# Uneven token split in the first expert product of four chunks: 512, 384, 448 and 320 tokens in place of 288

## The chip, the cores and the metric

The kernel runs on one core of a Trainium2 chip (trn2). The metric is the device time of one execution in microseconds; two runs before the change took 1317.12 and 1317.86 us, with a median of 1317.49 us. Lower is better. The core has a matrix engine (TensorE, shown as PE, its weight loads as PEld), three engines for element-wise work (VectorE as DVE, ScalarE as ACT, GpSimd as POOL), and SyncE (SP), whose queue issues almost all transfers. Every engine works through its own list of instructions in order and waits on semaphores for the others.

## The reference

Attention runs twice per head: 32 pack queries `p` attend to the keys and values, and then every token attends to the 32 packed results. What comes out, `x` (4608 tokens of 512 features), goes through a dense mixture of four experts:

```python
p_packed = sm_attn(p, k, v)
out = sm_attn(q, p_packed, p_packed)
...
for e in range(E):                       # E = 4, F = 1024
    h = np.maximum(x @ w1[e], 0.0)
    out += p[:, e:e + 1] * (h @ w2[e])
```

There are 8 batches of 576 tokens, 8 heads of 64 features, and everything is float32.

## The kernel before, in words

**Precision.** All large products are done in the rounded float type `float32r`. A float32 operand is split into a high part (a rounded copy, made on ScalarE by `hi_of`, line 103) and a low part (the rest, made on GpSimd or VectorE by `lo_of`, line 108), and each product is the sum of three: high by low, high by high, low by high.

**Units.** The hidden dimension of each expert is cut in two, which gives 8 chunks (`ch`) of 512 hidden columns. Batches go in pairs (`sb` = 0 to 3). One unit is one chunk of one batch, so there are 64 units, in the order pair, chunk, batch. The change touches pair `sb == 2` (batches 4 and 5) in the odd chunks 1, 3, 5 and 7, thus 8 units.

**The first expert product.** The second attention and `w1` are fused: `g_form` multiplies the packed results with `w1` into `ghl` (stationary operand, 128 x 128 pieces), and the attention weights `xh`, `xl` (256 rows by 576 tokens) are the moving operand. `mm1_group(u, kh, c)` computes one quarter of a unit's hidden block: two slices of 128 hidden columns (`fi`) for one half of the tokens (`c`, 288 of 576), by 12 matmuls of 128 x 288 into one PSUM tile `dbl` (two banks, room for 512 columns in each). Then one VectorE instruction (line 310) takes the maximum with zero, multiplies by the expert's probability and writes the block `ablk`. The four blocks of a unit are named like a 2 by 2 matrix: `a11`, `a12` (first token half, first and second pair of hidden slices) and `a21`, `a22` (second token half).

**The second expert product.** It is a Strassen product of 2 by 2 blocks: seven products in place of eight. `ORDER` lists the left operands: `a11`, `s3`, `s1`, `s2`, `a22`, `s4`, `a12`, where s1 = a21 + a22, s2 = s1 - a11, s3 = a11 - a21 and s4 = a12 - s2. `s_operand` makes a sum on VectorE (`sblk`, line 327), its high part on ScalarE and its low part on GpSimd (`st`, four buffers). `product` does 12 matmuls of 128 x 288 with `st` moving and the prepared `w2` combinations `tt` stationary, and VectorE adds the result to the accumulator `acc` (line 392).

**Order of the work.** The loop over units emits, after each product i of unit u, the operand of the product two places ahead (`LA = 2`, so s1 of the next unit is emitted after product 0 of that unit), and the next unit's first product by the table GROUPS: group (0,0) after product 1, (0,1) after 3, (1,1) after 4, (1,0) after 6. Where a step of the attention of the next pair, or a `g_form`, is due, it stands between them. A scheduler then fixes the order on each engine from these priorities, so an instruction can stand earlier or later than it was emitted. PSUM has four `dbl` tiles, which products, groups, `g_form` and the attention share.

The loop that calls the function is this, cut to the calls in question:

```python
GROUPS = {1: ((0, 0),), 3: ((0, 1),), 4: ((1, 1),), 6: ((1, 0),)}
...
        for i in range(NPROD):
            product(u, i)
            n = i + LA
            if n < NPROD:
                s_operand(u, n)
            elif nxt:
                s_operand(u + 1, n - NPROD)
            if nxt:
                for grp in (GROUPS_LATE if u == 1 else GROUPS).get(i, ()):
                    mm1_group(u + 1, *grp)
```

Of the kernel before, what the change touches and what calls it, by code (L numbers as in the profile page):

```python
# [8 lines left out]
F32 = mybir.dt.float32  # L9
F32R = mybir.dt.float32r  # L10
AF = mybir.ActivationFunctionType
ALU = mybir.AluOpType
# [4 lines left out]
P = 128  # L17
B, H, S, D = 8, 8, 576, 64
# [5 lines left out]
HS = S // 2  # L24
# [14 lines left out]
def attention_moe(ctx: ExitStack, tc: tile.TileContext, q, k, v, p, dp, w1, w2, out):  # L39
    nc = tc.nc  # L40
# [24 lines left out]
    def mm(**kw):  # L65
        on_pe(nc.tensor.matmul(**kw))  # L66
# [15 lines left out]
    def dbl():  # L82
        return ps_dbl.tile([P, 2, 512], F32, name="dbl")
# [199 lines left out]
    pbt = {}  # L283
# [5 lines left out]

    blocks = {}  # L290

    def mm1_group(u, kh, c):
        sb, ch, b = units[u]
        xh, xl = xs[b]
        ts = slice(c * HS, (c + 1) * HS)
        ps = dbl()
        for fi in range(2):
            f = 2 * kh + fi
            fs = slice(f * P, (f + 1) * P)
            n = 0  # L300
            for g in range(NG):
                ghl = gs[b, ch][g]
                for hl, rx in ((0, xl), (0, xh), (1, xh)):
                    mm(
                        out=ps[:, fi, 0:HS], lhsT=ghl[:, hl, fs], rhs=rx[:, g, ts],
                        start=n == 0, stop=n == 3 * NG - 1,
                    )
                    n += 1
        a = hpool.tile([P, 2, HS], F32, name="ablk", bufs=6)
        nc.vector.scalar_tensor_tensor(  # L310
            out=a, in0=ps[:, :, 0:HS], scalar=0.0,
            in1=pbt[b][:, ts].rearrange("p (o t) -> p o t", o=1).broadcast_to([P, 2, HS]),
            op0=ALU.max, op1=ALU.mult,
        )
        blocks[u, f"a{c + 1}{kh + 1}"] = a

    def s_operand(u, i):

# [152 lines left out]
    hpool = ctx.enter_context(tc.tile_pool(name="hpool", bufs=1, reuse_waits="tile"))  # L471
    with ExitStack() as first:
# [30 lines left out]
        for kh, c in ((0, 0), (0, 1), (1, 1), (1, 0)):  # L503
            mm1_group(0, kh, c)
# [33 lines left out]
    for u, (sb, ch, b) in enumerate(units):  # L538
# [25 lines left out]
        for i in range(NPROD):  # L564
# [6 lines left out]
# [3 lines that stand above are left out]
# [66 lines left out]
```

## Time and profile before

| what | value |
|---|---|
| runs, median | 1317.12 and 1317.86 us, 1317.49 us |
| span of the profiled execution | 1316.5 us |
| TensorE matmul (PE) busy | 1271.3 us, 97% |
| VectorE (DVE) busy | 955.5 us, 73% |
| GpSimd (POOL) busy | 859.4 us, 65% |
| ScalarE (ACT) busy | 477.4 us, 36% |
| granted TensorE clock, mean | 0.989 |

The span is the time from the first to the last instruction in one execution that the hardware profiler recorded; the runs' times include what lies around it. A group row of the profile gives line, engine, operation, the tiles written and read, the shape, the count, then the busy time and the mean duration of one, then the engine's idle time just before such instructions and what ended it. Matmuls overlap one another, so the mean duration of one (about 0.3 us) is longer than the distance from one to the next. The third pair's units lie between about 702 us and 1015 us of the span.

### The profile page before, as it was taken

To read this page: it belongs to the slowest core of one execution; us is meant where nothing else is said; L and a number is where in the kernel's file an instruction comes from. 1 tells how busy PE (TensorE), PEld (TensorE's weight loads), DVE (VectorE), ACT (ScalarE), POOL (GpSimd) and SP (SyncE) were. 2 spreads that over 40 slices of the span, in tenths; PEclk is the share of its full clock that TensorE was granted. 3 is DMA by queue.
4 is the path that set the end of the run, shared out by engine and by line. 5 is a ranking of instruction groups with operands and counts; after the bars stand their busy time and mean duration, and the time that the engine had idled before them with its cause. 6 is when DMAs were issued, how large, how long until landed. Compare 5 with 4: busy or idle time off the path is not lost.

```text
span 1316.5 us, 26695 instructions
## 1 busy us (share of the span) xinstructions
PE 1271.3 (97%) x10720; PEld 1178.2 (89%) x10720; DVE 955.5 (73%) x1334; ACT 477.4 (36%) x786; POOL 859.4 (65%) x576
## 2 busy tenths in 40 slices
PE   3999999999899999999999999999999999999997
PEld 2789898888899989999999998999999999999997
DVE  5585777899894676888687566699669466666668
ACT  2445434343335332333334433233323533323231
POOL 4878888688886445557578554566558655555556
PEclk8899999999999999999999999999999999999999
DMA  9786556445365445554335645443446443335422
GB/s 323 275 298 225 205 172 220 169 143 187 127 204 164 167 139 174 174 184 131 123 111 194 202 156 182 132 135 118 154 138 206 151 137 118 117 129 154 129 97 73
DMA packets 89979, 218.42 MB, mean 166 GB/s; under 512 B 9088, under 2 KB 31744, under 8 KB 89856
## 3 DMA queue, kind: packets, MB, share of 16 engines
q1 hardware_dynamic: 89184, 216.57, 49.4%
q8 instruction: 86, 1.41, 0.4%
q14 instruction: 37, 0.30, 0.1%
q10 hardware_dynamic: 672, 0.15, 0.1%
HBM read 177.81 MB, written 38.87 MB: 165 GB/s over the span
## 4 chain that ended last, share of the span: by engine, by line
PE 83%; DVE 9%; POOL 3%; DMA 2%; issue 1%; ACT 0%; DVEq 0%; SPq 0%; ACTq 0%; POOLq 0%
PE dbl L66 78%; PE dbl L74 5%; DVE sblk L327 2%; DVE acc L392 1%; DVE ablk L310 1%; POOL tt L108 1%; DVE acc L442 1%; DVE acc L407 1%; DMA pnd<-pb 1%; PE dbl L69 1%; POOL st L108 1%; POOL acc L442 1%; DVE ghl L108 1%; DMA td<-tt 0%; DVE nb L166 0%
## 5 line engine op out<-in xcount | busy, mean ns | idle before, releaser
L66 PEld LDWEIGHTS dbl<-st,tt 128*128 128x128 f32 x5376 | 730.9, 189 | 66.1 <-issue 31.1
L66 PE MATMUL dbl<-st,tt 128*128 128x288 f32 x5376 | 774.7, 298 | 9.6 <-DVE acc L392 3.7
L108 POOL TENSOR_TENSOR st<-sblk,st 128x576 fp32r<-128x576 f32 x256 | 396.8, 1556 | 220.2 <-ACT st L103 216.4
L66 PE MATMUL dbl<-xh,ghl 128*128 128x288 f32 x2048 | 419.0, 296 | 2.1 <-DVE ghl L108 2.1
L108 POOL TENSOR_TENSOR st<-ablk,st 128x576 fp32r<-128x576 f32 x192 | 288.2, 1504 | 180.5 <-ACT st L103 172.2
L392 DVE TENSOR_TENSOR acc<-dbl,acc 128x576 f32<-128x576 f32 x385 | 289.0, 752 | 121.3 <-PE dbl L66 119.7
L66 PEld LDWEIGHTS dbl<-xh,ghl 128*128 128x128 f32 x2048 | 331.5, 189 | 3.4 <-DVE ghl L108 3.4
L66 PE MATMUL dbl<-xl,ghl 128*128 128x288 f32 x1024 | 304.7, 298 | 17.7 <-POOL xl L108 13.5
L310 DVE SCALAR_TENSOR_TENSOR ablk<-dbl,pbt 128x576 f32<-128x576 f32 x256 | 192.6, 753 | 172.3 <-PE dbl L66 171.8
L103 ACT CAST st<-sblk 128x576 fp32r<-128x576 f32 x256 | 173.1, 676 | 300.8 <-DVE sblk L327 210.4
L66 PEld LDWEIGHTS dbl<-xl,ghl 128*128 128x128 f32 x1024 | 193.8, 189 | 21.0 <-POOL xl L108 14.7
L103 ACT CAST st<-ablk 128x576 fp32r<-128x576 f32 x192 | 129.8, 676 | 224.3 <-PE dbl L66 214.0
L103 ACT CAST ghl<-dbl 128x512 fp32r<-128x512 f32 x128 | 74.6, 586 | 146.5 <-PE dbl L74 91.7
L327 DVE TENSOR_TENSOR sblk<-ablk 128x576 f32<-128x576 f32 x128 | 118.3, 925 | 9.3
L108 DVE TENSOR_TENSOR ghl<-dbl,ghl 128x512 fp32r<-128x512 f32 x128 | 87.5, 685 | 10.2 <-ACT ghl L103 6.5
L74 PE MATMUL dbl<-wraw,ppbd 64*32 64x512 f32 x1024 | 72.9, 600 | 0.0
L327 DVE TENSOR_TENSOR sblk<-ablk,sblk 128x576 f32<-128x576 f32 x64 | 65.3, 1020 | 6.6 <-POOL st L108 0.9
L108 POOL TENSOR_TENSOR tt<-b,tt 128x512 fp32r<-128x512 f32 x42 | 59.3, 1419 | 5.6 <-ACT tt L103 5.5
L442 POOL TENSOR_TENSOR acc<-acc,acc 128x576 f32<-128x576 f32 x28 | 47.4, 1704 | 18.1 <-DVE acc L392 18.1
L327 DVE TENSOR_TENSOR sblk<-sblk,ablk 128x576 f32<-128x576 f32 x64 | 56.5, 883 | 1.7
L390 ACT COPY acc<-dbl 128x576 f32<-128x576 f32 x56 | 35.9, 641 | 47.4 <-PE dbl L66 46.5
L442 DVE TENSOR_TENSOR acc<-acc,acc 128x576 f32<-128x576 f32 x21 | 31.6, 1507 | 4.9 <-POOL acc L442 4.6
(76 smaller groups left out, 420.3 us busy)
## 6 DMA issues: line engine op xcount, KB each, us to landing
tt<-td SPq DMA_DIRECT2D x182, 512.0 KB, 4.4
wraw<-in_w SPq DMA_DIRECT2D x136, 256.0 KB, 3.2
td<-tt SPq DMA_DIRECT2D x56, 512.0 KB, 3.7
pbt<-pnd SPq DMA_DIRECT2D x32, 288.0 KB, 4.4
out<-acc SPq DMA_DIRECT2D x32, 288.0 KB, 2.3
kt<-in_k SPq DMA_DIRECT2D x14, 576.0 KB, 5.0
kt<-in_q SPq DMA_DIRECT2D x14, 576.0 KB, 5.5
vt<-in_v SPq DMA_DIRECT2D x15, 512.0 KB, 5.5
```

The source lines that it names most:

```text
L66: on_pe(nc.tensor.matmul(**kw))
L69: on_pe(nc.tensor.transpose(**kw))
L74: ins = nc.tensor.matmul(**kw).ins
L103: nc.scalar.copy(out=dst, in_=src)
L108: eng.tensor_tensor(out=dst, in0=src, in1=hi.bitcast(F32), op=ALU.subtract)
L310: nc.vector.scalar_tensor_tensor(out=a, in0=ps[:, :, 0:HS], scalar=0.0, in1=pbt[b][:, ts].rearrange("p (o t) -> p o t", o=1).broadcast_to( ...
L327: nc.vector.tensor_tensor(out=t, in0=blk(x), in1=blk(y), op=op)
L390: nc.scalar.copy(out=accs[b, i], in_=psv)
L392: nc.vector.tensor_tensor(out=accs[b, i], in0=psv, in1=accs[b, i], op=ALU.add)
L407: nc.vector.tensor_tensor(out=dst, in0=x, in1=y, op=op)
L442: eng.tensor_tensor(out=m[dst], in0=m[x], in1=m[y], op=op)
```

## The change

`mm1_group` no longer cuts the 576 tokens at 288 in the 8 units of pair 2 with an odd chunk. A table gives the width of the first piece: 512 in chunk 1, 384 in chunk 3, 448 in chunk 5 and 320 in chunk 7; the second piece is the rest: 64, 192, 128 and 256 tokens. The number of matmuls stays at 12 for a group and 48 for a unit, and so does the sum of their columns. The blocks `a11` to `a22` stay cut at 288, since the second product needs them so. So a group of the wide piece now writes a whole block of the first token half and a part of one of the second, by two VectorE instructions, and a group of the narrow piece writes the rest of that second block.

```diff
+    FIRST = {1: 512, 3: 384, 5: 448, 7: 320}
+
     def mm1_group(u, kh, c):
         sb, ch, b = units[u]
         xh, xl = xs[b]
-        ts = slice(c * HS, (c + 1) * HS)
+        cut = FIRST.get(ch, HS) if sb == 2 else HS
+        ts = slice(0, cut) if c == 0 else slice(cut, S)
+        w = ts.stop - ts.start
         ps = dbl()
...
                     mm(
-                        out=ps[:, fi, 0:HS], lhsT=ghl[:, hl, fs], rhs=rx[:, g, ts],
+                        out=ps[:, fi, 0:w], lhsT=ghl[:, hl, fs], rhs=rx[:, g, ts],
                         start=n == 0, stop=n == 3 * NG - 1,
                     )
                     n += 1
-        a = hpool.tile([P, 2, HS], F32, name="ablk", bufs=6)
-        nc.vector.scalar_tensor_tensor(
-            out=a, in0=ps[:, :, 0:HS], scalar=0.0,
-            in1=pbt[b][:, ts].rearrange("p (o t) -> p o t", o=1).broadcast_to([P, 2, HS]),
-            op0=ALU.max, op1=ALU.mult,
-        )
-        blocks[u, f"a{c + 1}{kh + 1}"] = a
+        for half in range(2):
+            lo, hi = max(ts.start, half * HS), min(ts.stop, (half + 1) * HS)
+            if lo >= hi:
+                continue
+            name = f"a{half + 1}{kh + 1}"
+            if (u, name) not in blocks:
+                blocks[u, name] = hpool.tile([P, 2, HS], F32, name="ablk", bufs=6)
+            nc.vector.scalar_tensor_tensor(
+                out=blocks[u, name][:, :, lo - half * HS:hi - half * HS], in0=ps[:, :, lo - ts.start:hi - ts.start],
+                scalar=0.0, in1=pbt[b][:, lo:hi].rearrange("p (o t) -> p o t", o=1).broadcast_to([P, 2, hi - lo]),
+                op0=ALU.max, op1=ALU.mult,
+            )
```

The names in the following lists are the program's: `dbl` is a PSUM tile, `xl` and `xh` the attention weights, `st` a split operand, `acc` an accumulator, and `a` the attention weights on their way through the softmax. The changed file is 9 lines longer, so line 310 is now 320, 327 is 336 and 392 is 401.

**TensorE, first unit of chunk 1.** These rows are the end of group (0,0), two products and the start of group (0,1):

```order
L66 MATMUL dbl<-xl_6506,ghl 128x512
L66 MATMUL dbl<-xh_6505,ghl 128x512 x2
L66 MATMUL dbl<-st,tt 128x288 x24
L66 MATMUL dbl<-xl_6506,ghl 128x64
L66 MATMUL dbl<-xh_6505,ghl 128x64 x2
```

Before, the same rows stand in the same sequence, with 128x288 in all of them; the widths differ.

**VectorE, between the first two units of chunk 5 (batch 4).** Here VectorE also does the softmax of the next pair's token attention (lines 235 to 241). The `sblk<-ablk` row is s1, `sblk<-sblk,ablk` is s2, and `sblk<-ablk,sblk` is s4. Before:

```order
L392 TENSOR_TENSOR acc_8979<-dbl,acc_8979 128x576
L236 TENSOR_SCALAR s_11019<-s_11019 128x18
L327 TENSOR_TENSOR sblk<-ablk 128x576
L392 TENSOR_TENSOR acc_8999<-dbl,acc_8999 128x576
L236 TENSOR_SCALAR s_11187<-s_11187 128x18
L237 RECIPROCAL s_11019<-s_11019 128x18
L327 TENSOR_TENSOR sblk<-sblk,ablk 128x576
L310 SCALAR_TENSOR_TENSOR ablk<-dbl,pbt 128x576
```

Now:

```order
L238 TENSOR_TENSOR a_10894<-a_10894,s_11029 128x576
L238 TENSOR_TENSOR a_10897<-a_10897,s_11198 128x576
L241 STREAM_TRANSPOSE at<-a_10894 128x576
L320 SCALAR_TENSOR_TENSOR ablk<-dbl,pbt 128x576
L320 SCALAR_TENSOR_TENSOR ablk<-dbl,pbt 128x2x160
L401 TENSOR_TENSOR acc_8537<-dbl,acc_8537 128x576
L336 TENSOR_TENSOR sblk<-ablk 128x576
L401 TENSOR_TENSOR acc_8558<-dbl,acc_8558 128x576
L241 STREAM_TRANSPOSE at<-a_10897 128x576
L336 TENSOR_TENSOR sblk<-sblk,ablk 128x576
```

The sums s1 and s2 stood ahead of the write-out of group (1,0); they now stand behind both of its write-outs, and behind the two multiplications of line 238 and one transposition.

**GpSimd, the same place.** The `xl` rows are the low parts of the next pair's attention weights; the rows are, in this order, `a11`, s3, `xl2`, s1, `xl3` and s2. Now:

```order
L108 TENSOR_TENSOR st_10989<-ablk_10853,st_10989 128x576
L108 TENSOR_TENSOR st_11010<-sblk_11008,st_11010 128x576
L108 TENSOR_TENSOR xl2_10330<-at_11055,xh2_10329 128x576
L108 TENSOR_TENSOR st_11052<-sblk_11050,st_11052 128x576
L108 TENSOR_TENSOR xl3_10334<-at_11270,xh3_10333 128x576
L108 TENSOR_TENSOR st_11075<-sblk_11073,st_11075 128x576
```

Before, the two `xl` rows stood further on, behind s1, s2, `a22`, s4 and `a12`; each now precedes one of the sums.

## The prediction

> **What bounds the kernel now.** I read the page first: the busy shares, the chain of work that ended last, and the costliest groups.
>
> ```profile
> span 1316.5 us, 26695 instructions
> PE 1271.3 (97%) x10720; PEld 1178.2 (89%) x10720; DVE 955.5 (73%) x1334; ACT 477.4 (36%) x786; POOL 859.4 (65%) x576
> PE 83%; DVE 9%; POOL 3%; DMA 2%; issue 1%; ACT 0%; DVEq 0%; SPq 0%; ACTq 0%; POOLq 0%
> L66 PE MATMUL dbl<-xh,ghl 128*128 128x288 f32 x2048 | 419.0, 296 | 2.1 <-DVE ghl L108 2.1
> L66 PEld LDWEIGHTS dbl<-xh,ghl 128*128 128x128 f32 x2048 | 331.5, 189 | 3.4 <-DVE ghl L108 3.4
> ```
>
> TensorE is busy nearly all the time and makes up 83% of the chain, so a nanosecond added to each of its matmuls arrives at the end, and one that another engine needs does not, until TensorE waits for it. Next I took the busy time by stretch for the third pair. Each row has a stretch, its length, the busy time and the number of instructions on PE, PEld, DVE, ACT and POOL, then the granted clock, the share of the DMA engines and GB/s.
>
> ```profile
> 740.00:780.00 40.00, 40.00 (x386) 37.43 (x385) 26.90 (x43) 14.27 (x25) 19.80 (x15) 1.00 0.53 174
> 820.00:860.00 40.00, 40.00 (x372) 36.83 (x371) 28.85 (x45) 12.98 (x20) 18.99 (x13) 1.00 0.50 159
> 860.00:900.00 40.00, 40.00 (x339) 37.19 (x338) 36.68 (x55) 14.28 (x22) 26.41 (x17) 1.00 0.39 124
> 940.00:980.00 40.00, 40.00 (x317) 38.00 (x316) 26.80 (x37) 12.28 (x19) 21.75 (x16) 1.00 0.43 133
> ```
>
> Here TensorE is full at a granted clock of 1.00, and VectorE has about a third of its time free, except between 860 and 900 us, where the softmax of the next pair loads it to 36.68 of 40 us. So two questions decide: what a narrow and a wide matmul cost, and whether a later block makes TensorE wait, above all near 900 us.
>
> The distance between matmuls comes from the timeline, where each row has its start, its duration and a count.
>
> ```profile
> 800.45 0.19 PEld L66 LDWEIGHTS dbl<-xl,ghl 128*128 128x128 f32 x1 [0.34 <-DVE nb L167]
> 800.56 0.33 PEld L66 LDWEIGHTS dbl<-xh,ghl 128*128 128x128 f32 x2
> 809.63 1.76 PE L66 MATMUL dbl<-st,tt 128*128 128x288 f32 x12
> 803.25 0.77 PE L69 MATMUL dbl<-ident,a 128*128 128x128 f32 x5
> ```
>
> Twelve matmuls of 288 columns take 1.76 us, of which the last alone is 0.30, so one follows another after (1.76 - 0.30) / 11 = 0.133 us. A group of the first product is the same, 1.60 us. The two loads at 800.45 and 800.56, the first ones after a wait, stand 0.11 us apart: that is how long a 128 x 128 weight load of the rounded type keeps the load path. Every matmul here has its own load, so no matmul can follow sooner than 0.11 us after the one before, however few columns it has, unless loads go faster in a stream than in this pair.
>
> **The change, part by part.** *Matmuls.* Nothing is removed: per chunk 96 wide or narrow matmuls stand for 96 of 288 columns, 48 pairs. If the distance is a constant plus so much for each column, a pair costs the same for every cut, 2 x 0.133 = 0.266 us, and only the floor of 0.11 us under the narrow ones adds time. The price of a column has to be bounded, since all these matmuls have 288:
>
> ```profile
> L74 PE MATMUL dbl<-wraw,ppbd 64*32 64x512 f32 x1024 | 72.9, 600 | 0.0
> L74 PE MATMUL dbl<-kt,pt 64*32 64x288 f32 x224 | 10.7, 436 | 5.2 <-DMA kt<-in_k 5.2
> ```
>
> At most it is 133 / 288 = 0.46 ns. For plain float32 these rows give (600 - 436) / 224 = 0.73 ns; if the rounded type took half of that, 0.37 ns. I take 0.42, between the two. Then 64 columns would follow after 133 - 0.42 x 224 = 39 ns, 128 after 66, 192 after 93, and 256 after 120. With the floor at 110 the loss of a pair is 71 ns (chunk 1), 44 (chunk 5), 17 (chunk 3) and 0 (chunk 7), together 132 ns, times 48 = **+6.3 us**. With 0.46 or 0.37 a column it would be 7.3 or 5.3. Bounds of the floor: below, none at all, 0 us. Above, 133 ns for every narrow matmul (if the present distance were already that of the loads): 94 + 67 + 40 + 13 = 214 ns, times 48 = 10.3 us. I take 110, because a load's own distance is the nearest row.
>
> The Trainium skill, in "TensorE: Matmul & The Clock Gate", section "LDWEIGHTS (loading the stationary operand)", gives a load P / 1.2 ns for P columns, an estimate of 107 ns for 128, and the 0.11 us between the two loads agrees; by it the sum would be 5.9 us in place of 6.3.
>
> *Write-outs.* Each of the 8 units has two more VectorE instructions. What an instruction costs beside its elements I take from these:
>
> ```profile
> L225 DVE STREAM_TRANSPOSE a<-dbl 128x288 f32<-128x288 f32 x32 | 12.8, 451 | 2.9 <-PE dbl L74 2.9
> L241 DVE STREAM_TRANSPOSE at<-a 128x576 f32<-128x576 f32 x16 | 12.3, 769 | 3.6 <-POOL a L238 3.0
> ```
>
> 288 elements more cost 318 ns, so 451 - 318 = 133 ns is fixed. Sixteen times 0.13 is 2.1 us of VectorE, spread over stretches with 11 to 13 free us in 40: nothing, since VectorE's free time there covers it; without that cover it would be the 2.1 us.
>
> *The wait that is added.* Block `a22` was complete after group (1,1); now its larger part comes with group (1,0), after product 6. So s1 = a21 + a22 can be formed only then, and product 2 of the unit needs it, three TensorE pieces later (products 0 and 1 and a group). The least roomy of the ordinary places is chunk 7, batch 4:
>
> ```profile
> 977.13 0.76 DVE L310 SCALAR_TENSOR_TENSOR ablk<-dbl,pbt 128x576 f32<-128x576 f32 x1 [0.82 <-PE dbl L66]
> 981.08 1.44 POOL L108 TENSOR_TENSOR st<-sblk,st 128x576 fp32r<-128x576 f32 x1
> 981.71 2.56 PE L66 MATMUL dbl<-st,tt 128*128 128x288 f32 x18
> ```
>
> From 977.13: write-outs 0.76 and, for 2 x 32 elements, 0.2; s1 0.75; ScalarE 0.7 and GpSimd 1.44, with three hand-overs of 0.1: ready at 981.3, before 981.71, when product 2 starts. The others have at least a microsecond more. Near 900 us it is different. Queued ahead of s1 on VectorE are now both multiplications of line 238, one transposition, both write-outs and an accumulator sum:
>
> ```profile
> 899.25 0.73 DVE L235 TENSOR_REDUCE s<-a 128x18 f32<-128x576 f32 x1
> 900.65 0.74 DVE L327 TENSOR_TENSOR sblk<-ablk 128x576 f32<-128x576 f32 x1
> 903.69 1.15 DVE L238 TENSOR_TENSOR a<-a,s 128x576 f32<-128x576 f32 x1
> 905.43 1.32 DVE L327 TENSOR_TENSOR sblk<-ablk,sblk 128x576 f32<-128x576 f32 x1
> 906.67 1.99 DVE L238 TENSOR_TENSOR a<-a,s 128x576 f32<-128x576 f32 x1
> 909.25 0.76 DVE L241 STREAM_TRANSPOSE at<-a 128x576 f32<-128x576 f32 x1
> 906.10 1.95 POOL L108 TENSOR_TENSOR st<-ablk,st 128x576 fp32r<-128x576 f32 x1
> 906.65 1.63 PE L66 MATMUL dbl<-st,tt 128*128 128x288 f32 x11
> ```
>
> Before, s1 was formed at 900.65 and product 2 started at 906.65. Now TensorE reaches that product later by three wide groups less two narrow ones: 3 x 12 x 67 ns - 2 x 12 x 23 ns = 1.8 us, at 908.5. VectorE's queue begins 0.8 us later (one wide group) and loses 0.7 in the two narrow write-outs, so line 235 starts at about 899.4. Behind it come two sums and four small ones (0.66 + 0.67 + 0.67 + 0.5 = 2.5, to 901.9), two multiplications (1.15 each, or 1.15 and 1.99: 2.3 to 3.1), a transposition 0.7, write-outs 0.67 and 0.45, a sum 0.67, and s1 itself, 0.74 to 1.32: it ends between 907.4 and 908.8. ScalarE 0.8 and GpSimd 1.44 follow: ready between 909.7 and 911.1, a wait of 1.2 to 2.6 us, 1.9 in the middle. For s2, a second transposition on VectorE and `xl3` on GpSimd stand between: 1.4 us more at product 3. Together I take **+3.3 us**, between 0 (a queue that runs faster) and 6 (twice as slow).
>
> At the last changed unit VectorE waits for GpSimd's sums of the finished batch:
>
> ```profile
> 996.66 1.97 DVE L442 TENSOR_TENSOR acc<-acc,acc 128x576 f32<-128x576 f32 x1 [0.66 <-POOL acc L442]
> 998.56 0.74 DVE L310 SCALAR_TENSOR_TENSOR ablk<-dbl,pbt 128x576 f32<-128x576 f32 x1
> 1002.23 2.95 PE L66 MATMUL dbl<-st,tt 128*128 128x288 f32 x21
> ```
>
> 998.56 + 0.74 + 0.2 + s1 0.75 to 1.1 + ScalarE 0.8 + GpSimd 1.44 = 1002.5 to 1002.8, against 1002.23: **+0.5 us**.
>
> **The sum.** 1316.5 + 6.3 + 3.3 + 0.5 = 1326.6 us of span. The median of the runs stands 1.0 us above the profiled span (1317.5 against 1316.5), so the time is **1327.6 us**, 0.8% over the present one.
>
> **Rivals.** *No floor.* If weight loads run far enough ahead in a stream, the narrow matmuls cost what their columns cost, pairs stay at 0.266 us, and without a wait on s1 the time is 1317.5, not slower than before; with the wait 1321. For it: the queue already loads one matmul ahead. Against it: loads are busy 89% of the span, and the first pair of them already stands 0.11 us apart. It decides if the distance of 64-column matmuls is under 60 ns. The same page of the Trainium skill, section "Back-to-back issue gap", gives in a stream of load and matmul about 131 ns for 512 columns and 81 for 128; by that estimate the 512/64 pairs would cost at most 212 ns, 54 less than now, a gain of 2.6 us; but the trace has 133 ns at 288 columns already, so I count it as a small part of this rival's chance.
>
> *A slower rate for narrow matmuls.* Plain float32 shows that there is more than one rate: the five transpositions at 803.25 take (0.77 - 0.29) / 4 = 120 ns for 128 columns or less, 0.94 ns a column. If the rounded type fell to that below its present width, 192 columns would follow after 180 ns and 256 after 240, and 64 and 128 after 110 and 120: losses of 71 + 54 + 87 + 120 = 332 ns, times 48 = 15.9 us, thus 1317.5 + 15.9 + 3.8 = 1337. At twice that price a column, which no row excludes, the losses are 120 - 39 = 81, 240 - 66 = 174, 360 - 93 = 267 and 480 - 120 = 360 ns: 42 us, 1363; if 256 columns still ran at the present rate, 25 us, 1346, slower by over 2%. For it: no row shows a rounded matmul under 288 columns. Against it: nothing in the trace changes rate with width.
>
> *Loads bound everything.* Floor 133 ns: 10.3 in place of 6.3, so 1331.6.
>
> *The wait spreads.* If the late s1 delays the accumulator sums behind it until PSUM runs out, each of the 8 units loses a microsecond or two: 1327.6 + 8 = 1336. Against it: TensorE waits nowhere in the stretches above, and VectorE has a third of its time.
>
> **How the numbers follow.** Chances: forecast 0.50, loads bound everything 0.13, no floor 0.13, slower rate 0.18 (0.07 of it over 1343.8), the wait spreads 0.06. 2%, or 26 us, is about what a measurement of this kernel can tell from no change. All but the worst slower rates lie within it: faster 0.01, same 0.92, slower 0.07. The range 1319 to 1340 takes in the forecast with both bounds of its floor, the plain rate and the spreading wait; what it leaves out is the lower end of "no floor" and the upper end of "slower rate".
>
> **What would show each step.** In the changed profile the matmul groups on line 66 split by shape. Twelve 64-column matmuls should take about 1.3 us between their first and the next piece of work, as should those of 128 and 192; those of 256 about 1.44; of 512 about 2.7 (12 x 227 ns). TensorE should wait about 2 us before product 2 and 1 us before product 3 in chunk 5, batch 4, for GpSimd, and hardly anywhere else. I am wrong if the narrow groups take 0.5 us (no floor), if 192 columns take longer than 288 (slower rate), or if waits stand in all 8 units.

## The result, and the profile after

The changed kernel took 1329.58 and 1333.17 us, median 1331.38 us, against 1317.49 before: a ratio of 1.0106 (95% interval 1.0073 to 1.0139). Timed again in five rounds beside the kernel before (the ninth run below), the ratio was 1.0121 (1.0104 to 1.0138). So it is slower by about 1%, 14 to 16 us. The profiled execution is the one of 1333.17 us, with a span of 1331.3 us, 14.8 us over that of before.

The page's rows that answer to those of before:

```profile
span 1331.3 us, 26724 instructions
PE 1280.7 (96%) x10720; PEld 1182.4 (89%) x10720; DVE 959.4 (72%) x1350; ACT 476.9 (36%) x786; POOL 860.9 (65%) x576
PE 81%; DVE 11%; POOL 4%; DMA 1%; issue 1%; ACT 0%; DVEq 0%; SPq 0%; ACTq 0%; POOLq 0%
```

TensorE is busy for 9.4 us more, and VectorE and GpSimd have gained 2 and 1 points of the chain: TensorE now also waits more. Where the time went is seen from the starts of the same product in the timelines of both kernels. The table gives the start of product 0 of the first unit of a stretch, and what the stretch took. The groups of a chunk run one unit ahead of its products, so each stretch begins before the chunk: that of chunk 1 with the last unit of chunk 0 (three units in all), the others with the first unit of the even chunk before (four units). The column "swapped" is the first experiment below.

| stretch holding the cut of | starts before, after | before | after | swapped | distances alone |
|---|---|---|---|---|---|
| everything ahead | 0, 0 | 722.05 | 719.72 | 719.38 | 0 |
| chunk 1 (512/64) | 722.05, 719.72 | 59.62 | 63.77 | 63.15 | +3.7 |
| chunk 3 (384/192) | 781.67, 783.49 | 81.35 | 82.27 | 82.27 | +0.9 |
| chunk 5 (448/128) | 863.02, 865.76 | 76.38 | 84.67 | 78.88 | +2.5 |
| chunk 7 (320/256) | 939.40, 950.43 | 75.60 | 79.41 | 76.53 | +0.05 |
| after the pair | 1015.00, 1029.84 | 301.5 | 301.5 | 301.6 | 0 |

So the pair itself took 17.2 us more (4.15 + 0.92 + 8.29 + 3.81), and 2.3 us were given back ahead of it, nearly all by chance, as shown further down. The last column is what the new distances between matmuls make of it. They are read from rows like these, of the wide and the narrow group of chunk 1 (a row holds one or two matmuls, and the starts of equal rows are three matmuls apart):

```profile
723.71 0.39 PE L66 MATMUL dbl<-xl,ghl 128*128 128x512 f32 x1
723.93 0.63 PE L66 MATMUL dbl<-xh,ghl 128*128 128x512 f32 x2
724.40 0.39 PE L66 MATMUL dbl<-xl,ghl 128*128 128x512 f32 x1
...
729.22 0.28 PE L66 MATMUL dbl<-xl,ghl 128*128 128x64 f32 x1
729.33 0.39 PE L66 MATMUL dbl<-xh,ghl 128*128 128x64 f32 x2
729.55 0.28 PE L66 MATMUL dbl<-xl,ghl 128*128 128x64 f32 x1
```

With 512 columns three matmuls take 724.40 - 723.71 = 0.69 us, 230 ns each; with 64 columns 0.33, 110 ns each. Over all groups the median distances are 231 (512), 207 (448), 173 (384), 147 (320), 120 (256), 111 (192), 112 (128) and 112 ns (64). The pairs lose 77, 53, 18 and 1 ns, times 48: 7.15 us in all. Nearly all of the other 10 us lies in two places.

**Chunk 5, batch 4.** The stages there, with the granted clock behind the busy times:

```profile
909.00:912.00 3.00, 2.77 (x15) 2.20 (x14) 3.00 (x4) 1.35 (x2) 1.54 (x2) 1.00 0.36 97
912.00:915.70 3.70, 1.80 (x12) 1.57 (x12) 3.09 (x5) 2.42 (x4) 3.70 (x3) 1.00 0.00 0
917.30:921.00 3.70, 3.70 (x23) 3.16 (x30) 1.20 (x3) 0.67 (x1) 3.70 (x3) 0.50 0.00 0
921.00:924.00 3.00, 3.00 (x24) 1.76 (x9) 1.48 (x2) 0.80 (x2) 0.17 (x1) 0.52 0.17 61
924.00:928.00 4.00, 4.00 (x35) 4.00 (x34) 1.94 (x4) 1.04 (x2) 1.42 (x1) 1.00 0.26 86
```

TensorE idles for 1.9 of the 3.7 us from 912, and then runs at half clock from 917 to 924 us, 6.8 us long. The timeline says what it waited for, and what half clock does:

```profile
908.39 1.21 DVE L336 TENSOR_TENSOR sblk<-ablk 128x576 f32<-128x576 f32 x1
910.46 1.43 POOL L108 TENSOR_TENSOR st<-sblk,st 128x576 fp32r<-128x576 f32 x1 [1.48 <-ACT st L103]
910.88 1.63 DVE L336 TENSOR_TENSOR sblk<-sblk,ablk 128x576 f32<-128x576 f32 x1
911.85 1.95 POOL L108 TENSOR_TENSOR xl<-at,xh 128x576 fp32r<-128x576 f32 x1
911.95 1.85 PE L66 MATMUL dbl<-st,tt 128*128 128x288 f32 x12 [0.23 <-POOL st L108]
912.62 0.68 ACT L103 CAST st<-sblk 128x576 fp32r<-128x576 f32 x1 [0.96 <-DVE sblk L336]
913.77 1.92 POOL L108 TENSOR_TENSOR st<-sblk,st 128x576 fp32r<-128x576 f32 x1
915.74 2.22 PE L66 MATMUL dbl<-st,tt 128*128 128x288 f32 x12 [1.94 <-POOL st L108]
917.76 0.31 PE L66 MATMUL dbl<-xl,ghl 128*128 128x128 f32 x1
918.30 0.41 PE L66 MATMUL dbl<-xl,ghl 128*128 128x128 f32 x1
918.94 0.41 PE L66 MATMUL dbl<-xl,ghl 128*128 128x128 f32 x1
920.35 1.96 PE L74 MATMUL dbl<-wraw,ppbd 64*32 64x512 f32 x16
```

Product 2 (911.95) waits shortly for the low part of s1, and product 3 (915.74) nearly 2 us for that of s2. The `xl` row on GpSimd holds this one up by only about 0.5 us, since ScalarE has the high part of s2 done at 913.30. The rest is that s2 itself is formed late on VectorE (910.88), and that the sum takes 1.63 us and its low part 1.92, in place of the usual 0.74 and 1.43. Then three matmuls of 128 columns take 918.94 - 918.30 = 0.64 us in place of 0.33, and the sixteen matmuls of line 74 take 1.96 in place of 1.09.

**Chunk 7, batch 5.** Here s1 is not what is late. The matmul shown is the sixth of the next pair's first group, the first that needs the low part of the second `ghl`. Before the change, then after it:

```profile
999.41 1.14 DVE L327 TENSOR_TENSOR sblk<-ablk,sblk 128x576 f32<-128x576 f32 x1
1000.47 0.68 DVE L108 TENSOR_TENSOR ghl<-dbl,ghl 128x512 fp32r<-128x512 f32 x1
1001.20 0.40 PE L66 MATMUL dbl<-xh,ghl 128*128 128x288 f32 x1 [0.29 <-DVE ghl L108]
```

```profile
1009.00 1.07 DVE L336 TENSOR_TENSOR sblk<-ablk 128x576 f32<-128x576 f32 x1
1010.11 1.88 DVE L336 TENSOR_TENSOR sblk<-sblk,ablk 128x576 f32<-128x576 f32 x1
1012.09 1.77 DVE L336 TENSOR_TENSOR sblk<-ablk,sblk 128x576 f32<-128x576 f32 x1
1013.79 0.68 DVE L108 TENSOR_TENSOR ghl<-dbl,ghl 128x512 fp32r<-128x512 f32 x1
1014.52 0.40 PE L66 MATMUL dbl<-xh,ghl 128*128 128x288 f32 x1 [2.45 <-DVE ghl L108]
```

Before, only s4 stood directly ahead of that low part, and TensorE waited 0.29 us. Now VectorE does s1, s2 and s4 one after another, the last two at more than twice the usual 0.74 us while GpSimd works beside it, and only then the low part of `ghl`, for which TensorE waits 2.45 us. Half clock follows again, 3.4 us from 1016.0.

**The 2.3 us ahead of the pair.** Half clock explains 2.05 of these. Two stretches of the kernel before, then the same two of the changed kernel:

```profile
330.00:335.70 5.70, 2.63 (x16) 2.19 (x17) 5.70 (x7) 2.98 (x5) 5.70 (x5) 1.00 0.00 0
335.70:339.20 3.50, 3.50 (x17) 3.50 (x17) 2.71 (x5) 1.17 (x2) 2.84 (x3) 0.51 0.44 169
```

```profile
330.00:335.70 5.70, 2.63 (x18) 2.20 (x18) 5.70 (x7) 2.98 (x5) 5.70 (x5) 1.00 0.00 0
335.70:339.20 3.50, 3.50 (x28) 3.50 (x27) 3.07 (x5) 1.93 (x3) 3.50 (x3) 1.00 0.39 147
```

In both kernels TensorE idles alike at 330 us, in the first pair, which the change doesn't touch; in the execution of before the clock then halved, and in the changed one it did not. It cost 2.05 us there. The code ahead of the pair is the same in every run of this document, and in all 13 profiled executions TensorE idles for 2.7 us at one go there; half clock followed in nine of them and not in four. So this difference is chance, and not the change.

### The profile page after: what moved, and what is told of

Same layout as the page of the kernel before. It is cut to its first block, busy times and chain, and to the rows that moved or that the text cites. A ratio compares the mean times of both kernels' runs of the same rounds, so it can differ in the third digit from the quotient of the medians.

```text
span 1331.3 us, 26724 instructions
## 1 busy us (share of the span) xinstructions
PE 1280.7 (96%) x10720; PEld 1182.4 (89%) x10720; DVE 959.4 (72%) x1350; ACT 476.9 (36%) x786; POOL 860.9 (65%) x576
## 4 chain that ended last, share of the span: by engine, by line
PE 81%; DVE 11%; POOL 4%; DMA 1%; issue 1%; ACT 0%; DVEq 0%; SPq 0%; ACTq 0%; POOLq 0%
PE dbl L66 76%; PE dbl L74 5%; DVE sblk L336 3%; POOL st L108 2%; DVE acc L401 1%; DVE ablk L320 1%; POOL tt L108 1%; DVE acc L416 1%; PE dbl L69 1%; DMA pnd<-pb 1%; POOL acc L451 1%; DVE acc L451 1%; DVE a L238 0%; DVE ghl L108 0%; DVE nb L166 0%
## 5 line engine op out<-in xcount | busy, mean ns | idle before, releaser
L66 PE MATMUL dbl<-xh,ghl 128*128 128x288 f32 (+4 forms) x2048 | 424.5, 299 | 4.3 <-DVE ghl L108 4.3
L66 PE MATMUL dbl<-xl,ghl 128*128 128x288 f32 (+4 forms) x1024 | 306.7, 300 | 19.5 <-POOL xl L108 14.7
L320 DVE SCALAR_TENSOR_TENSOR ablk<-dbl,pbt 128x576 f32<-128x576 f32 (+4 forms) x272 | 193.7, 717 | 174.7 <-PE dbl L66 174.2
L336 DVE TENSOR_TENSOR sblk<-ablk,sblk 128x576 f32<-128x576 f32 x64 | 68.1, 1065 | 5.6 <-POOL st L108 0.5
L103 ACT CAST tt<-b 128x512 fp32r<-128x512 f32 x42 | 25.2, 618 | 26.6 <-DVE b L373 11.4
```

The lines of the kernel that those rows point to most:

```text
L103: nc.scalar.copy(out=dst, in_=src)
L320: nc.vector.scalar_tensor_tensor(out=blocks[u, name][:, :, lo - half * HS:hi - half * HS], in0=ps[:, :, lo - ts.start:hi - ts.start], scal ...
L336: nc.vector.tensor_tensor(out=t, in0=blk(x), in1=blk(y), op=op)
```

## The experiments

My theory after the result: about 7 us are the floor that the weight load sets under narrow matmuls; the rest are sums that are formed too late in two places, and the half clock that follows the waits. The rivals: the widths cost all of it in some way; the additional write-outs load VectorE; the half clock comes from something else.

**Swapped pieces.** The narrow piece first, so that a22 is again complete after group (1,1).

```diff
         cut = FIRST.get(ch, HS) if sb == 2 else HS
+        cut = S - cut
         ts = slice(0, cut) if c == 0 else slice(cut, S)
```

> The same four cuts with the pieces swapped: the narrow piece comes first (64, 192, 128, 256 tokens in groups (0,0) and (1,0)), the wide one second. Matmul widths, their count and the number of write-outs are those of the change, but a22 is again complete after group (1,1). Theory (floor of the weight load 7.2 us, the rest late sums and the clock that falls after them): 7.2 us over the kernel before, about 1324.7 us, with no wait over 1 us in the changed units. Rival 1 (the widths themselves cost all of it): 14 us, as the change. Rival 2 (the 16 more write-outs load VectorE until TensorE waits): more than 10 us, with waits on VectorE in all changed units.

Measured: 1324.94 us, ratio 1.0055 (1.0042 to 1.0068), thus 7.2 us over the kernel before. The stage in question:

```profile
909.00:917.00 8.00, 8.00 (x63) 6.66 (x62) 6.24 (x11) 3.79 (x6) 8.00 (x6) 1.00 0.11 39
917.00:924.00 7.00, 7.00 (x49) 6.77 (x48) 6.28 (x10) 1.90 (x4) 4.28 (x4) 1.00 0.24 75
```

TensorE is full and the clock is whole. The table above shows the chunks: 3.53, 0.92, 2.50 and 0.93 us, the first three as the distances say. The widths and the number of write-outs are those of the change, so rivals 1 and 2 cannot explain more than about half of the loss; what is left in chunk 7 is one wait of 0.9 us.

**Half of the groups.** Only groups (0,0) and (0,1) cut, in the order of the change.

```diff
-        cut = FIRST.get(ch, HS) if sb == 2 else HS
+        cut = FIRST.get(ch, HS) if sb == 2 and kh == 0 else HS
```

> The cut of the change only in the groups of the first pair of hidden slices, (0,0) and (0,1); the other two groups stay at 288. Half the narrow matmuls, and a22 is complete after (1,1). Theory: half the floor, 3.6 us over the kernel before, 1321, no waits. Rival 1: half of 14, thus 7, 1324.5. Rival 2: half the write-outs, about 5 us with waits.

Measured: 1320.55 us, ratio 1.0021 (1.0011 to 1.0031), 1.4 to 4.1 us over. The theory's 3.6 lies within, 7 and 5 do not. In the trace, the four stretches took 1.76, 0.44, 1.23 and -0.5 us more. So it is the lateness of a22, not the wide-first order as such, that brings the waits.

**Chunk 5 alone, and with a filler.** The filler is 12 matmuls into a PSUM tile that nobody reads; apart from them the computation is the same.

```diff
-    FIRST = {1: 512, 3: 384, 5: 448, 7: 320}
+    FIRST = {5: 448}
```

```diff
         for i in range(NPROD):
+            if (sb, ch, b) == (2, 5, 4) and i == 3:
+                ps = dbl()
+                for n in range(12):
+                    mm(
+                        out=ps[:, n // 6, 0:HS], lhsT=gs[b, ch][0][:, 0, 0:P], rhs=xs[b][0][:, 0, 0:HS],
+                        start=n % 6 == 0, stop=n % 6 == 5,
+                    )
             product(u, i)
```

> Only chunk 5 is cut, at 448. Theory: floor 53 ns x 48 = 2.5 us, a wait of 2.6 us before products 2 and 3 of batch 4, and a half clock for 0, 3.4 or 6.8 us after it, which costs 0 to 3.4 us: 5.1 to 8.5 us over the kernel before, 1322.6 to 1326. Rival 1 (widths): the share of chunk 5 by its columns, a fifth of 14, thus 2.5 to 3.5 us, and no half clock.

> Chunk 5 cut at 448, and 12 matmuls of 288 columns more on TensorE between products 2 and 3 of batch 4, whose result nobody reads: 1.6 us of work placed where TensorE waits for s2. Theory (a wait of nearly 2 us brings the clock to half): the filler fills the wait, so the clock stays at 1.00 around that place, and the time is the same as or up to 3 us below that of chunk 5 alone. Rival (the half clock comes from something else, such as the narrow matmuls): the clock falls all the same, and the time is 0 to 1.6 us above that of chunk 5 alone.

Measured: 1323.17 us (ratio 1.0042, 1.0029 to 1.0056) without and 1322.72 us (1.0038, 1.0026 to 1.0051) with the filler. The times alone do not tell them apart. The traces do: without, then with the filler,

```profile
907.00:912.00 5.00, 2.84 (x18) 2.18 (x17) 4.20 (x6) 3.17 (x5) 5.00 (x4) 1.00 0.00 0
912.00:915.00 3.00, 3.00 (x15) 3.00 (x15) 0.17 (x1) 0.11 (x1) 3.00 (x3) 0.54 0.00 0
```

```profile
907.00:912.00 5.00, 4.77 (x29) 4.20 (x28) 5.00 (x7) 2.60 (x4) 3.56 (x3) 1.00 0.16 54
912.00:915.00 3.00, 2.63 (x20) 2.40 (x19) 1.07 (x2) 1.25 (x2) 3.00 (x2) 1.00 0.00 0
```

TensorE idles over 2 us of 5 in the first, and the clock halves; with the filler it does not. From unit to unit the stretch of chunk 5 took 6.7 us more than before without the filler and 5.2 with it, 12 matmuls included; 5.2 is what the distances (2.5) and the waits (2.6) come to without half clock. Half clock lasted 3.4 us here, and 6.8 in the whole change.

**Chunk 7 alone.**

```diff
-    FIRST = {1: 512, 3: 384, 5: 448, 7: 320}
+    FIRST = {7: 320}
```

> Only chunk 7 is cut, at 320 (256 columns cost no floor). Theory (in its second unit s1 and s2 now stand ahead of the low parts of ghl on VectorE, and the first group of the next pair waits for these): 2.2 us of wait, and a half clock of 0 to 3.4 us after it, together 2 to 4 us over the kernel before, 1320 to 1322. Rival (the wait came from how the earlier chunks had moved TensorE against the other engines): no wait over 1 us there, 1318.

Measured: 1320.24 us, ratio 1.0021 (1.0012 to 1.0031), 1.6 to 4.1 us over. In the trace the wait is there and half clock behind it:

```profile
1000.00:1004.00 4.00, 1.53 (x11) 1.42 (x11) 3.90 (x6) 2.40 (x4) 4.00 (x3) 1.00 0.87 175
1004.00:1007.40 3.40, 3.40 (x17) 3.40 (x16) 1.96 (x3) 0.67 (x1) 2.18 (x3) 0.50 1.08 401
```

The stretch took 3.8 us more, as in the whole change. So the wait comes from this chunk's own order on VectorE, and a cut whose narrow piece costs no floor at all still costs that much.

**Other widths.** Narrow piece first.

```diff
-    FIRST = {1: 512, 3: 384, 5: 448, 7: 320}
+    FIRST = {1: 480, 3: 352, 5: 416, 7: 336}
```

> Narrow piece first, with other widths: 96/480 in chunk 1, 224/352 in chunk 3, 160/416 in chunk 5, 240/336 in chunk 7. Theory (distance is 0.42 ns a column and 13 ns, and never under 112 ns): 96, 160 and 224 columns follow after 112 ns, 240 after 113; 480 after 214, 416 after 187, 352 after 160, 336 after 153; pairs lose 60, 33, 6 and 0 ns, 48 pairs each: 4.8 us, 1322.8. Rival (a slower rate below a width between 192 and 256): 224 or 240 columns take longer than 120 ns. Rival (the columns also cost more when wide): 480 columns over 225 ns.

Measured: 1321.95 us, ratio 1.0035 (1.0023 to 1.0047), 4.6 us over. The median distances are 112 (96), 112 (160), 113 (224) and 112 ns (240); 217 (480), 190 (416), 166 (352) and 154 (336). With 224 columns:

```profile
811.49 0.27 PE L66 MATMUL dbl<-xl,ghl 128*128 128x224 f32 x1
811.59 0.39 PE L66 MATMUL dbl<-xh,ghl 128*128 128x224 f32 x2
811.82 0.27 PE L66 MATMUL dbl<-xl,ghl 128*128 128x224 f32 x1
```

(811.82 - 811.49) / 3 = 0.11 us. The floor is flat from 64 to 240 columns, and there is no slower rate at any of the widths tried.

**Plain float32.** To test whether the floor belongs to the rounded type; the narrow matmuls read the same bits as plain float32, pieces swapped.

```diff
+                    as_is = (lambda t: t.bitcast(F32)) if w < HS else (lambda t: t)
                     mm(
-                        out=ps[:, fi, 0:w], lhsT=ghl[:, hl, fs], rhs=rx[:, g, ts],
+                        out=ps[:, fi, 0:w], lhsT=as_is(ghl[:, hl, fs]), rhs=as_is(rx[:, g, ts]),
```

> Narrow piece first with the widths of the change, and the narrow matmuls read the same bits as plain float32, not as the rounded type. Theory (the floor is the weight load of the rounded type, 0.11 us, while the loads of the plain-float transpositions stood 0.06 us apart): 64 columns come down from 112 ns to about 57 ns, 128 stay at about 110, and 192 and 256 rise to about 162 and 216, since plain float32 took 0.84 ns a column in the transpositions. Rival (the floor belongs to the matmul, or to a 128 x 128 array, whatever the type): 64 columns stay at 112 ns or more.

Measured: 1360.72 us, a single run. My expectation for 64 columns fell: each matmul became two passes with a weight load each, and a pass of 64 columns follows after 112 ns, as one of 128 does; 192 columns take 162 and 256 take 216 ns a pass. A load of 128 stationary columns takes as long in this type; the 0.06 us between loads of the transpositions is not the price of a load. It was the first distance alone: the five loads at 803.25 us in the trace of before follow one another after 59, 112, 109 and 109 ns. That left open whether the load or every matmul has the floor.

**Half the stationary columns.** Each narrow plain-float32 matmul in chunks 1 and 5 split in two, with 64 of the 128 stationary columns each.

```diff
+            for p0, np_ in ((0, P),) if w >= HS else ((0, D), (D, D)):
+                n = 0
...
-                        out=ps[:, fi, 0:w], lhsT=ghl[:, hl, fs], rhs=rx[:, g, ts],
+                            out=ps[p0:p0 + np_, fi, 0:w], lhsT=as_is(ghl[:, hl, f * P + p0:f * P + p0 + np_]), rhs=as_is(rx[:, g, ts]),
```

> Narrow piece first in chunks 1 and 5 alone (64 and 128 columns), read as plain float32, and each narrow matmul split in two that hold 64 of the 128 stationary columns, all six of the lower half before the six of the upper. With the whole 128 stationary columns in plain float32, each of the two passes of a matmul of 64 or of 128 columns followed after 112 ns. Theory (the floor is the weight load and goes with the stationary columns): passes of 64 moving columns come down to 54 to 60 ns each, those of 128 stay near 110 by their columns. Rival (a floor under every matmul, or by the moving type): 64 columns stay at 112 ns, and the groups take twice as long.

The two kernels' first narrow groups, 128 stationary columns and then 64 (the row of four is 3 distances and one duration, 0.275 and 0.222 us):

```profile
725.51 0.61 PE L66 MATMUL dbl<-xh,ghl 128*128 128x64 f32 x4
```

```profile
725.87 0.40 PE L66 MATMUL dbl<-xh,ghl 128*64 128x64 f32 x4
```

(0.61 - 0.275) / 3 = 112 ns, against (0.40 - 0.222) / 3 = 59 ns; with 128 moving columns it is 109, as their columns say. The moving columns are 64 in both, so the floor goes with the stationary columns, as a weight load does; a floor under every matmul, or by the moving type, is out. The whole took 1341.77 us, a single run, for the doubled passes. For the rounded type itself no run shows this.

**The change again, with fillers, and the fillers alone.** The second filler stands after product 1 in chunk 7, batch 5.

> The change once more, timed against the kernel before in five rounds. Theory: floor 7.2 us, late sums in chunk 5 with 2.6 us and in chunk 7 with 2.2 us, half clock behind them worth 0 to 5 us: 12 to 17 us over the kernel before. Rival (what the first pair of runs showed was partly chance): under 10 us.

Measured: 1333.42 us, ratio 1.0121 (1.0104 to 1.0138), 13.7 to 18.2 us over, so the rival's 10 is out. The half clocks are in the same two places, from 916.7 for 6.8 us and from 1015.7 for 3.4.

> The whole change, and twice 12 matmuls of 288 columns more on TensorE whose results nobody reads (3.2 us of work): before product 3 in chunk 5, batch 4, and after product 1 in chunk 7, batch 5, the two places where TensorE waited and the clock then fell. Theory (the clock falls because TensorE idles): no half clock near 917 and 1016 us, the waits of 2 us filled at no cost, so 3 to 5 us less than the change, 1328 to 1330. Rival (the clock falls for another reason): the half clock stays, and the time is that of the change or up to 3.2 us more.

Measured: 1331.07 us, ratio 1.0102 (1.0087 to 1.0118), 2.4 us under the change, with intervals that overlap, and above the 1328 to 1330 expected. In chunk 5 it went as expected: no half clock, and the stretch took 5.2 us more than before in place of 8.3, the filler's 1.6 us included. In chunk 7 it failed:

```profile
1007.99 1.74 PE L66 MATMUL dbl<-xh,ghl 128*128 128x288 f32 x12
1010.56 0.68 DVE L108 TENSOR_TENSOR ghl<-dbl,ghl 128x512 fp32r<-128x512 f32 x1
1011.16 0.74 DVE L401 TENSOR_TENSOR acc<-dbl,acc 128x576 f32<-128x576 f32 x1
1011.96 0.50 PE L66 MATMUL dbl<-xl,ghl 128*128 128x288 f32 x1 [2.22 <-DVE acc L401]
```

The filler took a PSUM tile, so the group behind it had to wait for the accumulator sum, which stands behind the same sums and `ghl` on VectorE. The wait of 2.2 us only moved, and half clock followed from 1012.1; the stretch took 5.2 us more than before, 1.4 more than without a filler. So in chunk 7 no filler shows that the idle brings the half clock; that rests on chunk 5 and on the swapped kernel, where the wait was 0.9 us and the clock stayed whole.

> The kernel before with the same 24 extra matmuls and no cut: what they cost where TensorE has no wait to hide them. Theory (TensorE sets the time here): 24 x 133 ns = 3.2 us over the kernel before, 1320.8. Rival (there is slack near these places that hides them in the kernel before too): under 1 us.

Measured: 1320.54 us, ratio 1.0019 (1.0010 to 1.0028), 2.5 us over (1.3 to 3.7), so the rival's 1 us is out; in the trace 1.6 and 1.3 us at the two places. So 12 matmuls cost 1.6 us near 908 us where TensorE has no wait, and save 3.1 us where it has one and the clock would fall.

## Why the prediction was right, and where it was wrong

The time, 1331.4 us, lies in the range, and 13.9 us more against the forecast 10.1 is the right sign with the right first term. But the sum was short. In the profile the changed pair took 17.2 us more: 7.15 by the distances, 0.45 in chunk 1, 2.6 and 3.1 in chunk 5 for the waits and the half clock, 2.2 and 1.6 in chunk 7 for the same two. Chance ahead of the pair gave back 2.3 in that execution, and the first two runs came out low: timed again, the change cost 15.7, not 13.9. The range holds either way. It is luck that the time is that of the rival "loads bound everything" (1331.6): the distances rule that rival out, so the time alone would have pointed to the wrong cause. And 2% was far more than is needed to tell a change from none: the intervals here reach 0.1 to 0.3% to each side.

By its steps:

- **The floor.** Forecast 110 ns from one pair of loads; measured 111 to 112 for 64, 128 and 192 columns, flat up to 240. The term was 6.3 and came out as 7.15, mostly since wide matmuls cost a little more than 0.42 ns a column: (231 - 133) / 224 = 0.44. That one pair of loads gave the right figure was partly luck: the first pair of the transpositions would have given 0.06 us. The experiment with half the stationary columns, in plain float32, shows that the floor goes with them. The Trainium skill's rule of P / 1.2 in "TensorE: Matmul & The Clock Gate", section "LDWEIGHTS (loading the stationary operand)", gives 107 ns for 128 columns, and by that estimate 53 for 64; measured were 112 and, in plain float32, 58 to 59.
- **The rivals on widths.** No floor: out, 64 columns follow after 112 ns. A slower rate: out, 192 and 224 columns follow after 111 and 113 ns. A floor of 133: out. The figure of about 131 ns for 512 columns in the same page's section "Back-to-back issue gap" does not hold here: 231 ns.
- **The write-outs.** Costed at nothing, rightly: the swapped kernel has as many and loses only what the distances say, but for 0.9 us.
- **The wait in chunk 5.** The place was right, and its size, 3.3 us forecast, was near: product 2 lost 0.4 us beyond the wider group and product 3 2.2. But the forecast had split it the other way, 1.9 and 1.4, since I let the two multiplications of line 238 run up to 3.1 us; they took 1.42 for both.
- **What failed: a wait was priced at its own length.** The step "Together I take +3.3 us" lacks what TensorE loses after an idle of 2 us. Half clock for 6.8 us cost about 3.1 more: 8.29 for the stretch, less 2.54 for the distances and 2.6 for the waits, is 3.15. The filler that took away the idle took away the half clock.
- **What failed as well: the last changed unit.** "998.56 + 0.74 + 0.2 + s1 ..." followed s1 to product 2 and asked for nothing else in VectorE's queue. s1 was indeed in time for its part; behind it, s2 and s4 delayed the low part of `ghl`, for which the next pair's first group waited. 0.5 us forecast, 3.8 measured, of which about 1.6 is half clock.
- **The wait that spreads.** Not in 8 units: chunk 1 lost 0.45 us beyond its distances and chunk 3 nothing.

On the clock the same page says, in its section "Part 1: The HAM clock gate (the "warmup" mystery)", that the clock is gated to half by how busy the array was in free-running windows of 3413 ns. That agrees with the trace: the stretches last 3.4 or 6.8 us, and the same idle at 330 us brought half clock in one execution and not in another. It asks for one idle window of about 3.4 us before the clock drops; here idles of 1.9 us (after 912 us) and 2.2 to 2.5 us (before 1015 us) were enough, so the measurement decides. The traces also bound what is harmless here: in all 13 profiled executions idles of 1.3 to 1.5 us near 215, 241, 267 and 272 us brought no half clock, while each of the seven of 1.9 to 2.5 us in and behind the changed units did. Between 1.5 and 1.9 us nothing was seen behind the start of the kernel.

## What to carry to other kernels

In these float32r products a matmul of less than about 240 moving columns costs as much as one of 240 when each brings its own 128-column weight load, so splitting a row of tokens unevenly pays for the narrow piece and gains nothing on the wide one. Price a wait of TensorE that nears 2 us at about double, since the clock may halve after it, for 3.4 us or more: here that added 1.6 to 3.1 us to waits of 2.2 to 2.6. And when a producer moves later in an in-order queue, follow every consumer behind it in that queue, not only its own.

## What had not been expected of the hardware

- An idle of 1.9 us in TensorE brought half clock for 6.8 us in two executions and for 3.4 in a third. An idle of 2.7 us in unchanged code, at 332 us, brought it in nine executions of 13 (2.05 us of difference).
- Sums on VectorE took 1.77 to 1.88 us in place of 0.74 while GpSimd worked on operands beside it (1009 to 1014 us).
- A matmul on plain float32 became two passes, each with its own load: 112 ns a pass up to 128 columns, 162 at 192 and 216 at 256, so 224 to 432 ns for one matmul, against 111 to 120 in the rounded type.
